# Narrow zero fills around the last pair's first decay, and expert 0's first product ahead of the branch

## The chip, the core and the metric

The kernel runs on one core of one Trainium2 chip. A core has five engines that work side by side and meet only through semaphores: PE (TensorE: matrix products and transposes), DVE (VectorE), ACT (ScalarE), POOL (GpSimd) and SP (SyncE, which here does nothing but issue DMAs). Each engine takes its instructions in the order of its own queue. The metric is the time of one execution on the device in microseconds (us), as the median of several runs.

## The reference

A gated linear recurrence is followed by a mixture of experts that keeps at most 80 tokens per expert:

```
a_t   = exp(8 * sigmoid(r_gate) * log(clip(sigmoid(a_param))))          # x, r_gate, i_gate: 4 x 5056 x 256
xg    = sqrt(max(1 - a_t * a_t, 1e-6)) * sigmoid(i_gate) * x
h     = a_t[:, t] * h + xg[:, t];  y[:, t] = h                            # for t in range(5056), float32

x = y.reshape(20224, 256);  logits = x @ w_gate                           # 8 experts
expert = argmax(logits);  gate = softmax(logits)[expert]
out = zeros(20224, 256)
for e in range(8):
    tok = the 80 tokens of expert e with the largest gate (all, if fewer)
    out[tok] = gate[tok] * (relu(x[tok] @ w1[e]) @ w2[e])                 # w1: 256 x 1024, w2: 1024 x 256
```

Nearly all of the 20.7 MB of `out` is zeros; only 640 rows of it are written by experts.

## The kernel before

**Tiles and units.** The 20224 tokens are cut into 20 pairs of 1024 tokens; pair 0 and the last pair, 19, are each worked in two units. The units of pair 19 are unit 20 (its tokens 0 to 511) and unit 21 (tokens 512 to 767); there are 22 units, 0 to 21. One big tile `Y` has 25 slots of 128 partitions x 2 x 1024 floats. A unit's three inputs are loaded into free slots, and its recurrence is computed in the slot of its own pair, `Y[:, p]`. The two index `h` of a slot is the half of the 256 channels.

**Order.** What every engine and SP do up to the routing is one list, `ORDER` (lines 31 to 51), written out by hand; each engine's queue has its own instructions in the order of that list. A letter is a step, followed by the unit and, after the point, the channel half: `r`, `i`, `x` issue the loads; `T` and `I` are the tanh of the gates on ACT (L117, L137); `A` transposes the r gate on PE into one PSUM buffer (L123); `E` is the decay, an exp on ACT from PSUM into the state `Y[:, p, h]` (L126); `Q` squares the decay on POOL (L129); `S` is the square root on ACT (L133), which needs another activation table than `E`; `U` multiplies gate and x on POOL (L140); `B` transposes that on PE (L147, L148); `N` scales it on DVE (L151); `Y` is the scan on DVE (L161), in place in the state; `l` computes the logits on PE (L241); `c` are the routing steps of a group of pairs (L245 to L271); `D` runs so many idle transposes on PE (L231); and `Z` issues a zero fill.

**Zero fills.** `zero_fill` (L203) writes the next rows of `out` with zeros from SBUF, by a DMA of SP's queue. Slot 19 is cleared once at the start. A wide fill (L209) writes 512 tokens, 512 KB, from all 1024 columns of `Y[:, 19, 0]`, 4 KB per partition. A narrow fill (L215) writes 256 tokens, 256 KB, from columns 768 to 1023 of the same row (`zero`), in pieces of 1 KB. No unit uses these columns, since the last pair has only 768 tokens. A wide fill reads where the decay `E20.0` will write. The flag `st['last']` is set when `E20.0` is put into the program; before it each `Z` is one wide fill, from then on two narrow ones. There are 28 wide and 23 narrow fills; the last narrow one is issued behind the first experts' weights.

**After the scans.** The routing picks each expert's best tokens: a chain of small DVE, POOL, ACT and PE steps up to `sel` (L449). Then `front` (L520) turns the choice into columns, keeps PE busy with 30 transposes (`keep_warm(WARM[3])`, L527, L352) and gathers the tokens of experts 0 and 1 into `XG`: `fetch` reads column numbers into registers (L505), and `copies` moves one token per instruction, 32 on ACT (L511), 24 on POOL and 24 on DVE (L512) for each expert. `rows_of_slots` (L513, five small DVE steps) follows. Ahead of `front` every engine reads a flag, and behind it there is a branch, `tc.If`: one side is a general way for many tokens in few rows, which is not taken here, the other is `experts` alone.

**Experts.** `experts` (L537) loops over `k`: `first(k)` is the product with `w1` into PSUM (L550, two halves), `relu(k, 0)` on ACT and `relu(k, 1)` on DVE write the hidden layer (L566, L565), `second(k)` is the product with `w2` (L560), `take` on ACT, `turn` on PE and `weigh` on DVE (L567, L571, L573) make rows, and `scatter` on POOL writes them (L576). In the same loop the tokens of expert `k + 2` are gathered and its weights loaded (L304, L307) into the buffers that expert `k` leaves.

Of the kernel before, what the change touches and what calls it, by code (L numbers as in the profile page):

```python
# [8 lines left out]
F32 = mybir.dt.float32  # L9
# [7 lines left out]
P = 128  # L17
# [26 lines left out]
A16.1 Z N15.0 D2 B15.1 E16.1 c2.1 c1.8 T17 Q16 l13 Y15.0 x17@23 Z I17 A17.0 N15.1 c2.2 B16.0 E17.0 r18@22 Y15.1 Z S16.1 A17.1 Z U17 c2.3 D4  # L44
B16.1 N16.0 l14 i18@24 E17.1 N16.1 x18@18 l15 T18 Y16.0 Q17 r19@20 c2.4 Y16.1 S17.1 D4 B17.0 c2.5 B17.1 N17.0 A18.0 i19@23 I18 c2.6 l16
N17.1 E18.0 U18 c2.7 c3.1 x19@21 c2.8 T19 A18.1 Z Y17.0 Z c3.2 Z E18.1 Z c3.3 I19 Q18 Y17.1 D14 B18.0 Z c3.4 Z c3.5 S18.1 B18.1 U19 c3.6
A19.0 i20@24 l17 N18.0 E19.0 N18.1 c3.7 Y18.0 D3 A19.1 r20@22 r21@22 E19.1 Z Z Z c3.8 Q19 D8 B19.0 I20 Z Y18.1 T20 T21 t D4 B19.1 S19.1 l18
x20@21 Z Z Z A20.0 Z Z E20.0 D9 A20.1 U20 i21@24 N19.0 E20.1 x21@21 N19.1 Z D5 A21.0 E21.0 Q20 Y19.0 Z S20.1 Z Y19.1 D23 B20.0 Z A21.1
E21.1 I21 N20.0 Z Q21 D5 B20.1 S21.1 c4.1 Y20.0 l19 U21 Z N20.1 c4.2 B21.0 Z Y20.1 c4.3 Z D5 B21.1 N21.0 l20 c4.4 N21.1 Y21.0 Z Y21.1 c4.5
D4 l21 Z c4.6 Z D2 c4.7 c5.1 c4.8 D2 c5.2 c5.3 c5.4 c5.5 c5.6 D25 c5.7 D7 c5.8  # L50
"""

def read_order():
# [11 lines left out]
def moe_kernel(ctx, tc, x, r_gate, i_gate, a_param, w_gate, w1, w2, out, capacity=80):  # L65
# [56 lines left out]
            at = 2 * g + (c0 - g) * D + h * P  # L122
            nc.tensor.transpose(pr[:, c0:min(n, g + 512):nb], rr[:, at:at + P], ident)  # L123
    def decay(u, h):
        if UNITS[u][0] == PAIRS - 1: st['last'] = True
        nc.scalar.activation(state(u, h), prs.pop((u, h))[:, :UNITS[u][2]], AF.Exp, scale=L[:, h:h + 1], bias=L[:, h:h + 1])  # L126
    def square(u):
        a = state(u)
# [74 lines left out]
    def zero_fill(k, wide=False):  # L203
        for _ in range(k):
            a = nz[0]
            if a >= N: return
            if wide and N - a >= 512 and not st.get('last'):
                nz[0] = a + 512
                nc.sync.dma_start(out[a:a + 512].rearrange("(p b) d -> p (b d)", p=P), Y[:, PAIRS - 1, 0])  # L209
                continue  # L210
            if wide:
                zero_fill(2)
                continue
            b = min(N, a + ZERO_TOKENS); nz[0] = b; m = (b - a) * D // P // ZC
            nc.sync.dma_start(out[a:b].rearrange("t d -> (t d)").rearrange("(p m c) -> p m c", m=m, c=ZC),  # L215
                              zero.unsqueeze(1).broadcast_to([P, m, ZC]))
# [65 lines left out]
    def gate_weights():  # L282
# [2 lines left out]
    tasks = {'r': lambda u: load('r', u, rf), 'i': lambda u: load('i', u, jf), 'x': lambda u: load('x', u, xf),  # L285
             'A': r_transposes, 'T': r_tanh, 'E': decay, 'Q': square, 'S': root, 'I': i_tanh, 'U': gated,
             'B': u_transposes, 'N': normed, 'Y': scan, 'c': lambda s, k: stages[k](s, width(s)), 't': early_top,
             'l': logits, 'D': idle, 'Z': lambda: zero_fill(1, True), 'w': gate_weights}
    with tc.manual_schedule(engines={E_.Activation, E_.PE, E_.DVE, E_.Pool, E_.SP}):
        for kind, nums in order: tasks[kind](*nums)  # L290
    mstack.close()
# [211 lines left out]
    def fetch(k, e):  # L503
        eng, et, a, b = SPAN[k]
        regs[k] = nc.values_load_multi_w_load_instructions(col[e:e + 1, a:b], engines=[et], min_val=0, max_val=PAIRS * 2 * C - C - 1,  # L505
                                                           skip_runtime_bounds_check_because="a token's column")[1]
    def copies(k, e, j0=0, j1=64):
        eng, et, a, b = SPAN[k]
        for j in range(a + j0, min(b, a + j1)):
            src = flat[:, bass.ds(regs[k][j - a], 2, step=C)]; dst = XG[:, e % 4, :, j]  # L510
            if k == 'A': eng.copy(dst, src)  # L511
            else: eng.tensor_copy(dst, src)  # L512
    def rows_of_slots():  # L513

        nc.vector.tensor_scalar(tk, AT[:, :E], -1.0, 0.0, op0=ALU.add, op1=ALU.max)
        nc.vector.tensor_scalar(un, tk, 11, 10, op0=ALU.logical_shift_right, op1=ALU.logical_shift_left)
        nc.vector.tensor_tensor(tk, tk, un, op=ALU.subtract)
        nc.vector.tensor_scalar(none, AT[:, :E], 0.0, 65536.0, op0=ALU.is_equal, op1=ALU.mult)
        nc.vector.tensor_tensor(sidx, tk, none, op=ALU.add)
    def front(ps):  # L520

        pc = ps.tile([E, CAP], F32, name="pv")
        nc.tensor.matmul(pc, comb[:3 * V, :E], chosen, start=True, stop=True)
        nc.vector.tensor_scalar(col, pc, -1.0, 0.0, op0=ALU.add, op1=ALU.max)
        pt = ps.tile([CAP, 2 * E], F32, name="sel")
        nc.tensor.matmul(pt, chosen, comb[:3 * V], start=True, stop=True)
        keep_warm(WARM[3], ps)  # L527
        for k in 'APV': fetch(k, 0)
        for k in 'APV': copies(k, 0)
        nc.vector.tensor_copy(AT, pt)  # L530
        for k in 'APV': fetch(k, 1); copies(k, 1)
        rows_of_slots()
    _, fv = nc.values_load_multi_w_load_instructions(flag, engines=[E_.PE, E_.DVE, E_.Activation, E_.Pool, E_.SP], min_val=0, max_val=P,
                                                     skip_runtime_bounds_check_because="a count of rows")
    with tc.manual_schedule(engines={E_.Activation, E_.PE, E_.DVE, E_.Pool, E_.SP}): front(ps_t)
    tstack.close()
    def experts(own):  # L537

# [4 lines left out]
        phs, pos, outs, sent = {}, {}, {}, []
        def hidden(e): return hbuf[e % 2].rearrange("p (c s) -> p c s", c=FC)
        def first(e, half):
            ph = phs[e, half] = ps_f.tile([P, FC // 2, CAP], F32, name="ph", bufs=3)
            for c in range(half * FC // 2, (half + 1) * FC // 2):
                for h in range(2):
                    for j in range(0, P, P // 2):
                        nc.tensor.matmul(ph[j:j + P // 2, c % (FC // 2)], w1v(e)[:, h, c * P + j:c * P + j + P // 2], XG[:, e % 4, h],  # L550
                                         start=(h == 0), stop=(h == 1), tile_position=(0, j))
            if half and e + 2 < E:
                for g in range(2): load_w1(e + 2, g)
# [9 lines left out]
        def relu(e, half):  # L563
            dst = hidden(e)[:, half * FC // 2:(half + 1) * FC // 2]
            if half: nc.vector.tensor_scalar_max(dst, phs.pop((e, half)), 0.0)  # L565
            else: nc.scalar.activation(dst, phs.pop((e, half)), AF.Relu)  # L566
        def take(e): nc.scalar.copy(turned[e % 2], pos.pop(e)[:, :, :CAP])  # L567
        def turn(e):

            outs[e] = ps_f.tile([CAP, 2 * P], F32, name="pd")  # L570
            for h in range(2): nc.tensor.transpose(outs[e][:, h * P:h * P + P], turned[e % 2][:, h], ident)  # L571
        def weigh(e):
            nc.vector.tensor_scalar_mul(res[e % 4][:CAP], outs.pop(e), AT[:, E + e:E + e + 1])  # L573
        def scatter(e):

            ins = nc.gpsimd.indirect_dma_start(out=out, out_offset=bass.IndirectOffsetOnAxis(ap=sidx[:, e:e + 1], axis=0),  # L576
                                               in_=res[e % 4][:CAP], in_offset=None, bounds_check=N - 1, oob_is_err=False)
            for other in sent: tc.declare_no_dep(ins.ins, other.ins, reason="rows of other tokens")
# [58 lines left out]
```

## Time and profile before

| what | value |
|---|---|
| median of 3 runs | 305.67 us (305.45 to 306.17) |
| the profiled execution: its time, its span | 306.08 us, 304.3 us |
| PE busy | 252.0 us (83% of the span) |
| ACT busy | 230.1 us (76%) |
| DVE busy | 210.5 us (69%) |
| POOL busy | 202.4 us (67%) |
| moved by DMA | 100.99 MB, mean 332 GB/s |

The times below are microseconds from the start of the span of the profiled execution. A row of the timeline gives start, duration, engine, line, operation, output and inputs, how many were merged, and in brackets the idle time of the engine before it and what ended that idle time. "SPq" is SP's queue: its rows are issues of DMAs, not the transfers. "issue" means that the profile shows nothing that the engine waited for. A row of the windows view gives, for one stretch, each engine's busy time, the clock granted to PE as a share of full speed, the busy share of the 16 DMA engines, and GB/s.

### The profile page before, as it was taken

The numbers are of one execution on the slowest core, as the hardware profiler recorded it, in microseconds if no ns is written. First come the engines' busy times: TensorE is split into PE (matmuls) and PEld (weight loads), VectorE is DVE, ScalarE is ACT, GpSimd is POOL, SyncE is SP. The second block draws the span as 40 slices with busy tenths as digits, with TensorE's granted clock in tenths as the row PEclk, the third lists the DMA queues.
The fourth block names the chain that finished last, engine by engine and source line by source line (L and its number), as shares of the span: only waits on it lengthen the run. The fifth ranks groups of instructions, "written<-read, shape, count | busy, mean of one in ns | idle before, by whom it ended". The sixth has DMA issues, their size and how long they took to land.

```text
span 304.3 us, 9900 instructions
## 1 busy us (share of the span) xinstructions
PE 252.0 (83%) x3748; PEld 228.0 (75%) x3748; DVE 210.5 (69%) x435; ACT 230.1 (76%) x443; POOL 202.4 (67%) x289
## 2 busy tenths in 40 slices
PE   4968899999899998999799798508979586996882
PEld 3767788898899897988788787407868486986871
DVE  2022069989999999999779889960779566566520
ACT  6999999999989999998998994607703366666510
POOL 2349999899999799899767488032305366777212
PEclk9999999999999999999999999955999787999997
DMA  6999999999999999889999999999997004999941
GB/s 235 407 412 408 409 411 407 408 408 408 407 416 412 365 364 323 325 313 381 409 357 401 310 369 416 408 363 329 308 346 259 1 4 167 300 382 384 360 150 32
DMA packets 38438, 100.99 MB, mean 332 GB/s; under 512 B 3056, under 2 KB 17264, under 8 KB 38384
## 3 DMA queue, kind: packets, MB, share of 16 engines
q1 hardware_dynamic: 38000, 99.63, 87.1%
q8 instruction: 31, 0.51, 0.7%
q0 software_dynamic: 384, 0.66, 0.7%
q14 instruction: 23, 0.19, 0.2%
HBM read 78.91 MB, written 21.36 MB: 330 GB/s over the span
## 4 chain that ended last, share of the span: by engine, by line
ACT 23%; DVE 18%; issue 14%; POOL 13%; DMA 12%; PE 11%; SPq 5%; POOLq 3%; DVEq 0%; ACTq 0%
DVE Y L161 8%; ACT Y L126 8%; POOL Y L512 6%; DVE pu L151 6%; ACT Y L117 5%; SPq L215 4%; ACT Y L133 4%; DMA out_dram<-Y 4%; DMA Y<-in_x_dram 4%; PE pr L123 3%; ACT Y L137 3%; POOLq L505 3%; DMA Y<-in_i_gate_dram 3%; POOL Y L129 2%; PE pu L147 2%
## 5 line engine op out<-in xcount | busy, mean ns | idle before, releaser
L140 POOL TENSOR_TENSOR Y<-Y 128x2048 f32<-128x2048 f32 (+2 forms) x22 | 90.9, 4142 | 20.7 <-DMA Y<-in_x_dram 14.4
L161 DVE TENSOR_TENSOR_SCAN Y<-Y,pu 128x1024 f32<-128x1024 f32 (+8 forms) x50 | 93.3, 1882 | 1.4 <-DMA out_dram<-Y 0.5
L129 POOL TENSOR_TENSOR Y<-Y 128x2048 f32<-128x2048 f32 (+2 forms) x22 | 71.6, 3260 | 28.7 <-ACT Y L126 18.7
L151 DVE SCALAR_TENSOR_TENSOR pu<-Y,pu 128x1024 f32<-128x1024 f32 (+2 forms) x44 | 48.6, 1111 | 52.8 <-PE pu L148 44.7
L148 PE MATMUL pu<-ident,Y 128*128 128x128 f32 x316 | 71.7, 274 | 3.4 <-POOL Y L140 3.4
L147 PE MATMUL pu<-ident,Y 128*128 128x128 f32 x316 | 72.6, 275 | 1.3 <-DVE Y L161 0.5
L123 PE MATMUL pr<-ident,Y 128*128 128x128 f32 x316 | 46.1, 289 | 24.3 <-ACT Y L126 20.0
L123 PEld LDWEIGHTS pr<-ident,Y 128*128 128x128 f32 x316 | 35.8, 146 | 32.6 <-ACT Y L126 27.7
L126 ACT ACTIVATE Y<-pr,tiny 128x1024 f32<-128x1024 f32 (+2 forms) x44 | 49.0, 1113 | 5.6 <-PE pr L123 5.3
L147 PEld LDWEIGHTS pu<-ident,Y 128*128 128x128 f32 x316 | 44.6, 141 | 4.8 <-issue 2.3
L148 PEld LDWEIGHTS pu<-ident,Y 128*128 128x128 f32 x316 | 44.6, 141 | 4.6 <-POOL Y L140 4.6
L231 PE MATMUL pl<-ident 128*128 128x128 f32 x287 | 42.6, 295 | 2.4 <-POOL ident masks.py:199 1.6
L137 ACT ACTIVATE Y<-Y 128x2048 f32<-128x2048 f32 (+2 forms) x22 | 38.2, 1736 | 4.7 <-DMA Y<-in_i_gate_dram 4.6
L511 ACT COPY Y<-Y 128x2 f32 x256 | 26.5, 191 | 18.5 <-issue 10.2
L117 ACT ACTIVATE Y<-Y 128x2048 f32<-128x2048 f32 (+2 forms) x22 | 38.1, 1736 | 2.7 <-DMA Y<-in_r_gate_dram 2.7
L241 PE MATMUL pl<-Y 128*32 128x64 f32 (+2 forms) x1344 | 39.0, 280 | 1.1 <-DVE lg L245 1.1
L231 PEld LDWEIGHTS pl<-ident 128*128 128x128 f32 x287 | 36.5, 154 | 3.2 <-POOL ident masks.py:199 1.6
L133 ACT ACTIVATE Y<-Y 128x2048 f32<-128x2048 f32 (+2 forms) x22 | 37.4, 1734 | 0.7 <-POOL Y L129 0.6
L241 PEld LDWEIGHTS pl<-Y 128*32 128x32 f32 x1344 | 33.9, 124 | 4.6 <-issue 3.2
L512 POOL COPY Y<-Y 128x2 f32 x192 | 24.4, 198 | 11.5 <-issue 6.9
L512 DVE COPY Y<-Y 128x2 f32 x192 | 22.6, 176 | 12.0 <-issue 12.0
L550 PE MATMUL ph<-Y 128*64 128x80 f32 x512 | 20.5, 233 | 4.9 <-issue 4.8
(126 smaller groups left out, 221.9 us busy)
## 6 DMA issues: line engine op xcount, KB each, us to landing
Y<-in_r_gate_dram SPq DMA_DIRECT2D x18, 1024.0 KB, 12.1
Y<-in_x_dram SPq DMA_DIRECT2D x18, 1024.0 KB, 9.3
Y<-in_i_gate_dram SPq DMA_DIRECT2D x18, 1024.0 KB, 9.7
Y<-in_moe_w_dram SPq DMA_DIRECT2D x32, 512.0 KB, 7.2
out_dram<-Y SPq DMA_DIRECT2D x28, 512.0 KB, 9.9
out_dram<-Y SPq DMA_DIRECT2D x23, 256.0 KB, 4.5
Y<-in_r_gate_dram SPq DMA_DIRECT2D x3, 512.0 KB
Y<-in_i_gate_dram SPq DMA_DIRECT2D x3, 512.0 KB
```

What stands on the lines that cost most here:

```text
L117: nc.scalar.activation(r, r, AF.Tanh, scale=0.5)
L123: nc.tensor.transpose(pr[:, c0:min(n, g + 512):nb], rr[:, at:at + P], ident)
L126: nc.scalar.activation(state(u, h), prs.pop((u, h))[:, :UNITS[u][2]], AF.Exp, scale=L[:, h:h + 1], bias=L[:, h:h + 1])
L129: nc.gpsimd.tensor_tensor(halves('r', u), a, a, op=ALU.mult)
L140: nc.gpsimd.tensor_tensor(i, i, flat('x', u), op=ALU.mult)
L147: nc.tensor.matmul(cols, xx[:, at:at + P], ident, start=True, stop=False, is_transpose=True)
L148: nc.tensor.matmul(cols, ii[:, at:at + P], ident, start=False, stop=True, is_transpose=True)
L151: nc.vector.scalar_tensor_tensor(pu, halves('r', u)[:, h], 0.5e-3, pu, op0=ALU.max, op1=ALU.mult)
L161: nc.vector.tensor_tensor_scan(y[:, s0:s1], y[:, s0:s1], q[:, s0:s1], init, op0=ALU.mult, op1=ALU.add)
L231: for _ in range(n): nc.tensor.transpose(spare, ident, ident)
L241: nc.tensor.matmul(pl[32 * j:32 * j + 32, s % 2, c0:c0 + n // NR], gates(h, b), Y[:, p, h, o + 4 * j + b:o + n:NR], start=(b == 0 and h == ...
L512: else: eng.tensor_copy(dst, src)
```

## The change

The nine `Z` that stand between the loads `r21` and the decay `E20.0` in the order, and all behind it, become `z`: two narrow fills each. The flag `st['last']` goes away; a `Z` is always a wide fill. So nine wide fills become eighteen narrow ones, and the fills behind `E20.0` are narrow as before.

In `front`, `rows_of_slots` moves ahead of the gather of expert 1, `first(0)` and `relu(0)` are computed there, between the gather of expert 0 and that of expert 1, and `keep_warm` runs 26 transposes in place of 30. The hidden layer of expert 0 goes to columns 1024 to 1663 of slot 24 (`scr`) in place of `rows`; its PSUM tile comes from the pool in front of the branch. The loop in `experts` skips `first` and `relu` for expert 0, and issues the loads of `w1` from the loop body.

```diff
-WARM = (4, 45, 6, 30)
+WARM = (4, 45, 6, 26)
...
-A19.0 i20@24 l17 N18.0 E19.0 N18.1 c3.7 Y18.0 D3 A19.1 r20@22 r21@22 E19.1 Z Z Z c3.8 Q19 D8 B19.0 I20 Z Y18.1 T20 T21 t D4 B19.1 S19.1 l18
-x20@21 Z Z Z A20.0 Z Z E20.0 D9 A20.1 U20 i21@24 N19.0 E20.1 x21@21 N19.1 Z D5 A21.0 E21.0 Q20 Y19.0 Z S20.1 Z Y19.1 D23 B20.0 Z A21.1
-E21.1 I21 N20.0 Z Q21 D5 B20.1 S21.1 c4.1 Y20.0 l19 U21 Z N20.1 c4.2 B21.0 Z Y20.1 c4.3 Z D5 B21.1 N21.0 l20 c4.4 N21.1 Y21.0 Z Y21.1 c4.5
+A19.0 i20@24 l17 N18.0 E19.0 N18.1 c3.7 Y18.0 D3 A19.1 r20@22 r21@22 E19.1 z z z c3.8 Q19 D8 B19.0 I20 z Y18.1 T20 T21 t D4 B19.1 S19.1 l18
+x20@21 z z z A20.0 z z E20.0 D9 A20.1 U20 i21@24 N19.0 E20.1 x21@21 N19.1 z D5 A21.0 E21.0 Q20 Y19.0 z S20.1 z Y19.1 D23 B20.0 z A21.1
+E21.1 I21 N20.0 z Q21 D5 B20.1 S21.1 c4.1 Y20.0 l19 U21 z N20.1 c4.2 B21.0 z Y20.1 c4.3 z D5 B21.1 N21.0 l20 c4.4 N21.1 Y21.0 z Y21.1 c4.5
...
-        if UNITS[u][0] == PAIRS - 1: st['last'] = True
...
-            if wide and N - a >= 512 and not st.get('last'):
+            if wide and N - a >= 512:
...
+             'l': logits, 'D': idle, 'Z': lambda: zero_fill(1, True), 'z': lambda: zero_fill(2), 'w': gate_weights}
...
+    hbuf = [rows[:, :FC * CAP], rows[:, FC * CAP:2 * FC * CAP], scr[:, 1024:1024 + FC * CAP]]
+    def hidden(e): return hbuf[e % 2 if e else 2].rearrange("p (c s) -> p c s", c=FC)
...
-        for k in 'APV': fetch(k, 1); copies(k, 1)
         rows_of_slots()
+        for half in range(2): first(0, half, ps, 2)
+        for k in 'APV': fetch(k, 1)
+        for half in range(2): relu(0, half)
+        for k in 'APV': copies(k, 1)
...
-            if k: take(k - 1)
-            if 0 < k < E - 1: copies('A', g - 1, 16, 24)
-            first(k, 0); relu(k, 0)
-            if 0 < k < E - 1: copies('A', g - 1, 24); copies('V', g - 1, 20)
-            first(k, 1); relu(k, 1)
-            if k: turn(k - 1); weigh(k - 1)
+            if k:
+                take(k - 1)
+                if k < E - 1: copies('A', g - 1, 16, 24)
+                first(k, 0, ps_f, 3); relu(k, 0)
+                if k < E - 1: copies('A', g - 1, 24); copies('V', g - 1, 20)
+                first(k, 1, ps_f, 3); relu(k, 1)
+                turn(k - 1); weigh(k - 1)
             if g < E:
+                for h in range(2): load_w1(g, h)
                 for q in 'APV': fetch(q, g)
                 copies('A', g, 0, 16); copies('V', g, 0, 20); copies('P', g)
```

`first` and `relu` keep their bodies; `first` gets the PSUM pool and its number of buffers as arguments.

## Rows read from the trace of the kernel before

**Rows 1.** The page: GB/s in 40 equal slices of the span.

```profile
GB/s 235 407 412 408 409 411 407 408 408 408 407 416 412 365 364 323 325 313 381 409 357 401 310 369 416 408 363 329 308 346 259 1 4 167 300 382 384 360 150 32
```

**Rows 2.** The timeline from 193 to 222 us, units 20 and 21.

```profile
197.94 2.34 POOL L140 TENSOR_TENSOR Y<-Y 128x1024 f32<-128x1024 f32 x1 [7.89 <-DMA Y<-in_x_dram]
...
204.75 1.28 ACT L126 ACT_TABLE_LOAD   x1 [9.06 <-DMA out_dram<-Y]
...
208.94 1.89 POOL L129 TENSOR_TENSOR Y<-Y 128x1024 f32<-128x1024 f32 x1 [8.66 <-issue]
...
211.47 1.06 ACT L133 ACTIVATE Y<-Y 128x1024 f32<-128x1024 f32 x1
...
213.32 0.27 PE L147 MATMUL pu<-ident,Y 128*128 128x128 f32 x1
...
214.46 0.69 DVE L151 SCALAR_TENSOR_TENSOR pu<-Y,pu 128x512 f32<-128x512 f32 x1 [11.89 <-PE pu L148]
214.62 0.56 ACT L126 ACTIVATE Y<-pr,tiny 128x256 f32<-128x256 f32 x1 [0.79 <-PE pr L123]
...
215.08 0.62 ACT L137 ACTIVATE Y<-Y 128x512 f32<-128x512 f32 x1
...
216.62 1.30 POOL L140 TENSOR_TENSOR Y<-Y 128x512 f32<-128x512 f32 x1
217.01 0.63 ACT L133 ACTIVATE Y<-Y 128x512 f32<-128x512 f32 x1
...
219.25 0.30 PE L147 MATMUL pu<-ident,Y 128*128 128x128 f32 x1
```

**Rows 3.** The timeline of SP's queue from 184 to 226 us.

```profile
184.46 2.98 SPq L209 DMA_DIRECT2D out_dram<-Y  x4
189.78 0.34 SPq L109 DMA_DIRECT2D Y<-in_x_dram  x1
190.17 4.61 SPq L209 DMA_DIRECT2D out_dram<-Y  x5
195.25 0.53 SPq L113 DMA_DIRECT2D Y<-in_i_gate_dram  x1
196.53 0.39 SPq L113 DMA_DIRECT2D Y<-in_x_dram  x1
197.74 21.71 SPq L215 DMA_DIRECT2D out_dram<-Y  x22
219.55 1.05 SPq L304 DMA_DIRECT2D Y<-in_moe_w_dram  x2
```

**Rows 4.** Tile Y, loads of unit 21 (195 to 197 us): from issue to landing.

```profile
DMA to landing us min/median/max: 9.5/9.8/10.1
```

**Rows 5.** Line L215, fills from 199 and from 207.8 us: ns of an issue, landing.

```profile
L215 SPq DMA_DIRECT2D out_dram<-Y x5: 933/1318/1543, 199.0 to 204.8; - x5
...
L215 SPq DMA_DIRECT2D out_dram<-Y x12: 680/716/737, 207.8 to 216.1; - x12
...
DMA to landing us min/median/max: 3.8/3.9/4.4
```

**Rows 6.** Windows: engines busy, PE clock, DMA share, GB/s.

```profile
184.40:197.00 12.60, 9.42 (x128) 8.34 (x126) 12.19 (x16) 7.04 (x6) 4.92 (x3) 1.00 1.02 411
207.00:219.00 12.00, 12.00 (x131) 11.32 (x131) 4.03 (x5) 9.29 (x11) 4.34 (x4) 0.78 0.99 330
```

**Rows 7.** The timeline from 247 to 262 us, experts 0 and 1.

```profile
247.94 2.43 PE L550 MATMUL ph<-Y 128*64 128x80 f32 x64 [0.19 <-issue]
...
249.57 3.33 ACT L511 COPY Y<-Y 128x2 f32 x32 [1.83 <-PE ph L550]
...
253.19 0.44 ACT L566 ACTIVATE rows<-ph 128x320 f32<-128x320 f32 x1 [0.29 <-issue]
...
253.68 3.88 PE L560 MATMUL po<-rows,Y 128*64 128x80 f32 x64 [3.31 <-ACT rows L566]
...
257.61 0.29 ACT L567 COPY Y<-po 128x160 f32<-128x160 f32 x1 [0.61 <-PE po L560]
```

More of the change, by code (lines that the diff above doesn't have):

```diff
@@ L46 @@
 N17.1 E18.0 U18 c2.7 c3.1 x19@21 c2.8 T19 A18.1 Z Y17.0 Z c3.2 Z E18.1 Z c3.3 I19 Q18 Y17.1 D14 B18.0 Z c3.4 Z c3.5 S18.1 B18.1 U19 c3.6
-A19.0 i20@24 l17 N18.0 E19.0 N18.1 c3.7 Y18.0 D3 A19.1 r20@22 r21@22 E19.1 Z Z Z c3.8 Q19 D8 B19.0 I20 Z Y18.1 T20 T21 t D4 B19.1 S19.1 l18
-x20@21 Z Z Z A20.0 Z Z E20.0 D9 A20.1 U20 i21@24 N19.0 E20.1 x21@21 N19.1 Z D5 A21.0 E21.0 Q20 Y19.0 Z S20.1 Z Y19.1 D23 B20.0 Z A21.1
-E21.1 I21 N20.0 Z Q21 D5 B20.1 S21.1 c4.1 Y20.0 l19 U21 Z N20.1 c4.2 B21.0 Z Y20.1 c4.3 Z D5 B21.1 N21.0 l20 c4.4 N21.1 Y21.0 Z Y21.1 c4.5
-D4 l21 Z c4.6 Z D2 c4.7 c5.1 c4.8 D2 c5.2 c5.3 c5.4 c5.5 c5.6 D25 c5.7 D7 c5.8
+A19.0 i20@24 l17 N18.0 E19.0 N18.1 c3.7 Y18.0 D3 A19.1 r20@22 r21@22 E19.1 z z z c3.8 Q19 D8 B19.0 I20 z Y18.1 T20 T21 t D4 B19.1 S19.1 l18
+x20@21 z z z A20.0 z z E20.0 D9 A20.1 U20 i21@24 N19.0 E20.1 x21@21 N19.1 z D5 A21.0 E21.0 Q20 Y19.0 z S20.1 z Y19.1 D23 B20.0 z A21.1
+E21.1 I21 N20.0 z Q21 D5 B20.1 S21.1 c4.1 Y20.0 l19 U21 z N20.1 c4.2 B21.0 z Y20.1 c4.3 z D5 B21.1 N21.0 l20 c4.4 N21.1 Y21.0 z Y21.1 c4.5
+D4 l21 z c4.6 z D2 c4.7 c5.1 c4.8 D2 c5.2 c5.3 c5.4 c5.5 c5.6 D25 c5.7 D7 c5.8
 """
@@ L287, in moe_kernel @@
              'B': u_transposes, 'N': normed, 'Y': scan, 'c': lambda s, k: stages[k](s, width(s)), 't': early_top,
-             'l': logits, 'D': idle, 'Z': lambda: zero_fill(1, True), 'w': gate_weights}
+             'l': logits, 'D': idle, 'Z': lambda: zero_fill(1, True), 'z': lambda: zero_fill(2), 'w': gate_weights}
     with tc.manual_schedule(engines={E_.Activation, E_.PE, E_.DVE, E_.Pool, E_.SP}):
@@ L519, in rows_of_slots, with first, relu @@
         nc.vector.tensor_tensor(sidx, tk, none, op=ALU.add)
+    hbuf = [rows[:, :FC * CAP], rows[:, FC * CAP:2 * FC * CAP], scr[:, 1024:1024 + FC * CAP]]
+    phs = {}
+    def hidden(e): return hbuf[e % 2 if e else 2].rearrange("p (c s) -> p c s", c=FC)
+    def first(e, half, ps, bufs):
+        ph = phs[e, half] = ps.tile([P, FC // 2, CAP], F32, name="ph", bufs=bufs)
+        for c in range(half * FC // 2, (half + 1) * FC // 2):
+            for h in range(2):
+                for j in range(0, P, P // 2):
+                    nc.tensor.matmul(ph[j:j + P // 2, c % (FC // 2)], w1v(e)[:, h, c * P + j:c * P + j + P // 2], XG[:, e % 4, h],
+                                     start=(h == 0), stop=(h == 1), tile_position=(0, j))
+    def relu(e, half):
+        dst = hidden(e)[:, half * FC // 2:(half + 1) * FC // 2]
+        if half: nc.vector.tensor_scalar_max(dst, phs.pop((e, half)), 0.0)
+        else: nc.scalar.activation(dst, phs.pop((e, half)), AF.Relu)
     def front(ps):
@@ L539, in experts @@
         ps_f = own.enter_context(tc.tile_pool(name="ps_f", bufs=1, space=bass.MemoryType.PSUM))
-        hbuf = [rows[:, :FC * CAP], rows[:, FC * CAP:2 * FC * CAP]]
         turned = [scr[:, (8 + 2 * k) * CAP:(10 + 2 * k) * CAP].rearrange("p (h s) -> p h s", h=2) for k in range(2)]
         res = [scr[:, 1024:1280], scr[:, 1280:1536], scr[:, 1536:1792], scr[:, 1792:2048]]
[L543 to L553, printed above, removed]
+        pos, outs, sent = {}, {}, []
         def second(e, half):
@@ L562, in second @@
             if e + 2 < E: load_w2(e + 2, half)
[L563 to L566, printed above, removed]
         def take(e): nc.scalar.copy(turned[e % 2], pos.pop(e)[:, :, :CAP])
```

## The prediction

> **What bounds the kernel now.** I read the page's GB/s line first [rows 1]. Up to about 190 us every slice but the first stands between 310 and 416 GB/s; the transfers set the pace there, and the change leaves that stretch alone. From 236 to 251 us the line shows 1 and 4 GB/s: the transfers have run dry, and the kernel is a chain of small computing steps that nothing but their own start can shorten. So the question is what decides when that chain starts. It starts with the last scans, those of units 20 and 21, so the next view is the timeline from 193 to 222 us [rows 2].
>
> There ACT is idle for 9.06 us, to 204.75, and what ends it is a transfer to `out`. The table load behind the wait is that of the decay `E20.0`, which writes the part of slot 19 that the wide fills read. ACT had been free since 195.69 (204.75 - 9.06). Behind it everything of unit 20 is late: POOL idles 8.66 us before `Q20` at 208.94, DVE 11.89 us before `N20.0` at 214.46. SP's queue [rows 3] shows the nine wide fills, four issued from 184.46 and five from 190.17, around the load `x20`, then `i21` and `x21`, then 22 narrow ones one after another to 219.45.
>
> The last view is the timeline around the branch [rows 7]. PE ends `first(0)` at 250.37 (247.94 + 2.43) and begins `second(0)` at 253.68, 3.31 us later, released by `relu(0, 0)`. That stands behind the 32 copies of expert 1 on ACT's queue, which began at 249.57.
>
> **The change part by part.**
>
> *The wait of the decay.* With the fills from the columns 768 to 1023, no transfer behind the r loads reads what `E20.0` writes. The wide fills that remain ahead of it are issued before `r21`, and so ahead of the 184.46 of [rows 3]; with 10.1 us to landing, the longest of [rows 4], they are in by 194.6. `E20.0`'s table load can begin when ACT is free, at 195.69: a gain of 9.06 us at this step. From there to `B20.0` (213.32) the path is decay, transposes, idle transposes on ACT and PE, and moves as a block: `B20.0` at 204.26, and `N20.0`, whose transposes end just ahead of it, at 205.40.
>
> *What is late next.* Two things could hold up this block. The first is `x20`, which POOL waits for at 197.94 before `U20` (2.34 us), with `Q20` behind it in the queue. Four wide fills ahead of it become eight narrow ones. A pair of narrow fills moves the same 0.524 MB as a wide one. At 411 GB/s, the rate of the stretch with wide fills, that is 1.28 us; at 330 GB/s, the stretch of narrow ones [rows 6], it is 1.59. Four times the difference of 0.31 is 1.25 us. `x20` lands at 199.2, `U20` ends at 201.5, `Q20` (1.89) at 203.4, the root `S20` (1.06 [rows 2]) at 204.5. `N20.0` needs it at 205.40: 0.9 us to spare, so this costs nothing.
>
> The second is `i21` and `x21`. They land 10.1 and 9.5 us after their issue [rows 4], at 205.35 and 206.03, behind all nine. At 0.31 each they come 2.8 us later, at 208.15 and 208.8. ACT is ready for `I21` at 206.4 (`E21.1` before: 214.62 + 0.56 [rows 2]; less 9.06 it would end at 206.1; behind the root at 204.5 and a table load of 1.28 it ends at about 206.4), so now `I21` waits for its load: it ends at 208.8 in place of 215.70. `U21` then begins at 208.9 (before: 216.62), the root `S21` about 210.1 (217.01). The last transposes `B21.1` stood 2.63 us behind the start of `U21`, at 219.25, released by the scan of unit 20; that scan now ends 9.06 earlier, so `U21` decides: 208.9 + 1.30 for itself and about 1.1 for eight transposes of its first half and the idle ones gives 211.3, a gain of 8.0. That is the lower end. The upper comes from the issue of narrow fills in a full stream, 716 ns each [rows 5]: two are 1.43 us, nine pairs cost 9 x 0.15 = 1.4 us, `x21` lands at 207.4, and the gain is all of 9.06. The row of 330 GB/s holds thin moments that the second one has not; I take the middle, **8.5 us**.
>
> On rate the Trainium skill (DMA: Bandwidth & Descriptors, Specifications) gives 512 B as the smallest transfer for line rate, and pieces of 1 KB are above that. By that rule the fills would cost nothing, and this step would give 9.06. The trace says otherwise: 330 against 411 GB/s [rows 6].
>
> *What the narrow fills push back.* The first weights were issued at 219.55 [rows 3], behind all fills, and come 1.4 to 2.8 us later. `first(0)` used them at 247.94, now at about 239.4; landing within 10.1 us of the issue, the longest of [rows 4], they would be there by 232.5. The dry stretch from 236 [rows 1] covers that. Without this cover every microsecond would be paid.
>
> *From the scans to the gather* no instruction is changed, and the chain moves as it is.
>
> *The product and relu ahead of the branch.* `first(0)` still waits for the last copy of expert 0 on ACT, which ended at 247.74 (249.57 - 1.83 [rows 7]); PE began at 247.94. Four idle transposes fewer therefore give nothing, and cost nothing as long as PE's clock stays up. The two relus come ahead of the copies of expert 1. ACT reaches its own after `fetch`, at 249.57, with the first half of the product (half of 2.43) done at 249.2; DVE's follows the second half at 250.4 and takes about 0.5, so `second(0)` may begin at about 250.9: 2.7 us earlier. But ACT's queue holds the same work as before, with relu (0.44) and copies (3.33) exchanged. `take(0)` stands behind `fetch` and copies for expert 2, and only its own wait for PE, 0.61 us at 257.61, goes away. `relu(1, 0)` is behind it, and with that `second(1)`. So of 2.7 us PE keeps 0.6. DVE's copies of expert 1 come later by five small steps and a relu, some 2 us; the product that needs them comes behind `second(0)`, which took 3.88, so from 254.8. They meet it closely; the loss, if any, is that 0.6 and some tenths. Bounds: 0 and 2.7; I take **0.6**, the row of ACT's wait.
>
> *At nothing:* `load_w1` keeps its place in SP's queue, and for expert 2 it still waits for `first(0)`. The new place of the hidden layer overlaps the buffers that `weigh(0)` writes, but that comes behind `second(0)` in any case.
>
> The sum against the profiled execution: 306.08 - 8.5 - 0.6 = 297.0. That execution was 0.41 us above the median of the runs, 305.67; against the median it is **296.6 us**.
>
> **The rivals.**
>
> *The fills eat most of it.* The rate of narrow fills is not all: five of the issues took a median of 1.32 us and up to 1.54 [rows 5], while wide ones and loads were still ahead of them. The 22 of [rows 3] took 0.99 each. Eighteen at that are 17.8 us against 7.6 for the nine wide, 10.2 later. But the loads then stand in a shorter queue and land in 4.4 us rather than 10.1 [rows 4, 5], so `i21` is 4.5 later, at 209.9, and `x21` near 210.5. `U21` starts at 210.6, the gain falls to 6.2, and the time is 298.9 with the second edit's 0.6, 299.5 without. It decides when `x21` lands later than 208.8. At 1.54 for every one of the eighteen (27.7 us, 20.1 later) `x21` would land near 221, 4.4 after `U21`'s start before, and the time would be 309.5: one of the rivals on the slow side.
>
> On many small transfers the Trainium skill (DMA: Bandwidth & Descriptors, Anatomy of one DMA, told there for the path of GpSimd) counts some 2 us fixed for each. Paid in a row by nine more fills that is an estimate of 18 us, close to the 20.1 of this slow end. The rows show issues 0.72 us apart that land after 3.9 [rows 5]: they overlap, and the cost is not paid one by one.
>
> *PE keeps the lead.* If ACT is not what holds `second(1)`, all of 2.7 us stays: 305.67 - 8.5 - 2.7 = 294.5. Against it stands the 0.61 us of [rows 7]: ACT had hardly any waiting to lose.
>
> *The second edit loses its gain*, since the copies of expert 1 come late: 0 in place of 0.6, up to 1 lost; 297.2 to 298.2.
>
> *Slower: the wait stays and grows.* The narrow fills read the same row `Y[:, 19, 0]` as the wide ones, at other columns. If the waits are set for the row and not for the columns, `E20.0` waits for the eighteenth narrow fill, which lands 1.4 to 2.8 us later than the ninth wide one did, near 207.5 in place of 204.75. With 0.6 from the second edit that gives 307.9. Below 0.6 us of delay it would be no change. The rows don't decide between the two readings: whatever writes this row behind the 22 narrow fills of [rows 3] comes late enough for those ahead of it to have landed. The program names columns that don't overlap, and I hold it unlikely.
>
> **How the numbers follow.** What this measurement can tell from no change is about 0.2%, 0.6 us. The forecast, 296.0 (9.06) to 297.1 (8.0) and 0.6 to either side, so 295.4 to 297.7, has a chance of 0.55. The fills eating most of it has 0.18 (298 to 301), their slow end 0.02, PE keeping the lead 0.1 (294 to 295.4), the second edit losing its gain 0.08 (297.2 to 298.6), the wait that stays 0.05, and 0.02 is left for no change. The prediction is that of the forecast, 296.6. To leave out no more than 2 in 10 the range runs from 294.4 to 300.0. Faster by more than 0.2% is 0.91 (0.55, 0.18, 0.1 and 0.08), within it 0.02, slower 0.07.
>
> **What would show it right or wrong.** In the profile after, ACT's idle time before the table load of `E20.0` should be nearly gone, with `E20.0` at about 197. `I21` should be released by its load, at about 207 to 208.2, and `N20.0` begin near 205.4. The last `B21.1` should be near 210.3 to 211.3. `second(0)` should begin within 0.7 us of the end of `first(0)`, and `second(1)` be released by ACT. The forecast is wrong if `E20.0` is still released by a transfer to `out`, if `x20` lands after 200.1 (the spare 0.9 us gone), if `first(0)` waits for weights, or if the gaps of PE in the later experts grow.

## The result, and the profile after

| what | before | changed |
|---|---|---|
| median of 4 runs | 305.92 us (305.45 to 307.17) | 294.47 us (291.80 to 295.59) |
| ratio, 95% interval | | 0.961 (0.954 to 0.968) |
| the profiled execution: time, span | 306.08, 304.3 us | 295.59, 293.8 us |

The change gains about 11.5 us by the medians, where 9.1 were forecast. The two profiled executions differ by 10.49 us. The means, standard errors and ratios below leave out runs more than 1.5% above the fastest of the same kernel in their group, the medians do not; with those runs in, no mean of the last table moves by more than 0.3 us. The timeline of the changed kernel over units 20 and 21 answers to [rows 2]:

```profile
195.72 1.28 ACT L125 ACT_TABLE_LOAD   x1
197.01 0.78 ACT L125 ACTIVATE Y<-pr,tiny 128x512 f32<-128x512 f32 x1
198.38 2.35 POOL L139 TENSOR_TENSOR Y<-Y 128x1024 f32<-128x1024 f32 x1 [8.63 <-DMA Y<-in_x_dram]
...
200.31 2.92 PE L230 MATMUL pl<-ident 128*128 128x128 f32 x23
...
202.61 1.06 ACT L132 ACTIVATE Y<-Y 128x1024 f32<-128x1024 f32 x1 [0.19 <-POOL Y L128]
...
204.20 0.70 DVE L150 SCALAR_TENSOR_TENSOR pu<-Y,pu 128x512 f32<-128x512 f32 x1 [1.62 <-PE pu L147]
...
205.88 0.63 ACT L136 ACTIVATE Y<-Y 128x512 f32<-128x512 f32 x1 [0.34 <-DMA Y<-in_i_gate_dram]
...
206.71 1.29 POOL L139 TENSOR_TENSOR Y<-Y 128x512 f32<-128x512 f32 x1
...
208.98 0.27 PE L146 MATMUL pu<-ident,Y 128*128 128x128 f32 x1
```

The table load of `E20.0` has no idle time before it any more; it begins at 195.72, which is 9.03 us earlier than in [rows 2]. `N20.0` begins at 204.20 (10.26 earlier), `I21` at 205.88, released by its load after 0.34 us. The last `B21.1` begins at 208.98 (10.27 earlier). The timeline of SP's queue, which answers to [rows 3]:

```profile
184.09 8.15 SPq L214 DMA_DIRECT2D out_dram<-Y  x8
192.35 0.99 SPq L109 DMA_DIRECT2D Y<-in_x_dram  x1
193.39 8.04 SPq L214 DMA_DIRECT2D out_dram<-Y  x10
201.47 0.70 SPq L113 DMA_DIRECT2D Y<-in_i_gate_dram  x1
202.26 0.63 SPq L113 DMA_DIRECT2D Y<-in_x_dram  x1
202.94 17.29 SPq L214 DMA_DIRECT2D out_dram<-Y  x22
220.32 1.38 SPq L303 DMA_DIRECT2D Y<-in_moe_w_dram  x2
```

`i21` is issued 6.2 us later than before and lands only some 0.5 later. Line L113's loads from 201 to 203 us:

```profile
DMA to landing us min/median/max: 4.3/4.4/4.4
```

Issue to landing is 4.4 us, against 9.5 to 10.1 in [rows 4]. The later issue and the shorter way to landing nearly cancel. PE's timeline around the branch answers to [rows 7]:

```profile
238.10 2.43 PE L527 MATMUL ph<-Y 128*64 128x80 f32 x64 [1.49 <-DVE lg L517]
240.62 2.44 PE L565 MATMUL po<-Y 128*64 128x80 f32 x64
243.75 2.43 PE L527 MATMUL ph<-Y 128*64 128x80 f32 x64 [0.69 <-DVE Y L511]
247.51 0.42 PE L572 MATMUL pd<-ident,Y 128*80 128x128 f32 x2 [1.33 <-ACT Y L568]
248.60 4.05 PE L565 MATMUL po<-rows,Y 128*64 128x80 f32 x64 [0.67 <-ACT rows L532]
252.48 2.38 PE L527 MATMUL ph<-Y 128*64 128x80 f32 x64
```

`second(0)` stands directly behind `first(0)` and takes 2.44 us; in [rows 7] it took 3.88 after a gap of 3.31. But in this execution `second(1)`, with the same 64 matmuls, takes 4.05. The windows view, columns as in [rows 6], shows why: first the stretch of `second(1)`, then `first(0)` to `first(2)`, and last the same stretch of the kernel before.

```profile
248.60:252.48 3.88, 3.88 (x64) 3.88 (x66) 2.58 (x19) 2.30 (x24) 2.67 (x21) 0.56 0.66 207
...
238.10:252.48 14.38, 11.60 (x258) 10.92 (x260) 8.65 (x69) 8.68 (x83) 9.19 (x72) 0.88 0.69 225
247.94:262.31 14.37, 11.06 (x259) 10.62 (x260) 8.05 (x60) 8.24 (x75) 9.15 (x72) 0.88 0.51 163
```

The granted clock is 0.56 in the first row: most of this product ran at the lower level (1.2 GHz). So the execution profiled here shows the first edit's gain and hardly any of the second's: from `first(0)` to `first(2)` it took 14.38 us, and the kernel before 14.37 (247.94 to 262.31). The difference between the kernels' medians is larger than that of these two executions, and the experiments had to show from where.

### The profile page after: what moved, and what is told of

The parts are those of the page before. It is cut to its first block, busy times and chain, and to the rows that moved or that the text cites. A ratio compares the mean times of both kernels' runs of the same rounds, so it can differ in the third digit from the quotient of the medians.

```text
span 293.8 us, 9900 instructions
## 1 busy us (share of the span) xinstructions
PE 250.0 (85%) x3744; PEld 227.2 (77%) x3744; DVE 210.2 (72%) x435; ACT 229.5 (78%) x443; POOL 202.2 (69%) x289
## 4 chain that ended last, share of the span: by engine, by line
ACT 28%; PE 17%; issue 14%; DVE 12%; POOL 12%; DMA 11%; POOLq 3%; ACTq 1%; SPq 1%; DVEq 0%
ACT Y L125 8%; ACT Y L132 6%; DVE Y L160 5%; POOL Y L511 5%; ACT Y L117 5%; PE pr L123 4%; DMA Y<-in_r_gate_dram 4%; DVE pu L150 4%; DMA Y<-in_x_dram 4%; DMA Y<-in_i_gate_dram 3%; PE pu L146 3%; PE pu L147 3%; ACT Y L136 3%; ACT L125 3%; PE pl L240 3%
```

## The experiments

The kernel before ran beside each group of experiments. Over all groups, the runs of the first table with them, its mean is 305.33 us (standard error 0.19), that of the changed kernel 293.81 (0.29). Both vary by some microseconds from run to run, so single microseconds below come from such means.

**Each edit alone, and the price of narrow fills.** `fills_only` is the kernel before with the fills' edit; `product_only` is the changed kernel with the old order and flag; `after_again` is the changed kernel unaltered, on the same chip; `all_narrow` makes every wide fill of the order narrow, 19 more.

```diff
 # fills_only, on the kernel before                       # in ORDER from r21@22 on: Z -> z
-        if UNITS[u][0] == PAIRS - 1: st['last'] = True
-            if wide and N - a >= 512 and not st.get('last'):
+            if wide and N - a >= 512:
 # all_narrow, on the changed kernel                      # in all of ORDER: Z -> z
-... i11@13 D7 B7.0 Y6.1 I9 A9.1 Z
+... i11@13 D7 B7.0 Y6.1 I9 A9.1 z
```

> The fills alone; expert 0's product stays behind the branch and 30 idle transposes are kept. Theory A (the forecast's first term was too small: the narrow fills hold the loads back by half a microsecond and not by 1.4 to 2.8, and the rest of the gain is PE's clock in this stretch): 9.8 us less than before, which is where first(0) stood in the profile after, so about 296.1. Theory B (the first term was right at 8.5, the second edit gives the rest): about 297.4.

> The product and relu ahead of the branch alone, the fills wide as before. Theory A (ACT's queue gives the lead back within two experts): 0.6 us less than before, 305.3. Theory B (PE keeps the lead of about 3 us that second(0) has): near 302.8.

> The changed kernel unchanged, for a closer interval on the same chip as the two halves. If the halves add up, its gain over before is the sum of theirs, 10.4 by theory A of both; if it is near 12, something is gained only by both together.

> The changed kernel with the 19 wide fills that remain made narrow as well, 38 of them in the stretch where transfers set the pace. Theory A (a pair of narrow fills costs 1.36 us where a wide one costs 1.25, as the landings in the profile after show): 19 x 0.11 = 2.1 us more than the changed kernel. Theory B (the 330 GB/s of the forecast): 19 x 0.31 = 5.9 us more.

| kernel | median us | ratio to before, 95% |
|---|---|---|
| fills_only | 296.20 | 0.969 (0.964 to 0.973) |
| product_only | 303.09 | 0.988 (0.982 to 0.994) |
| after_again | 292.88 | 0.959 (0.954 to 0.963) |
| all_narrow | 294.22 | 0.963 (0.958 to 0.969) |

Both edits gain alone, and the two gains add up: 9.4 (305.56 - 296.20) and 2.5 us make 11.9, and together they give 12.7. The second edit is worth several times the 0.6 us forecast. Nineteen more fills in two pieces cost 1.3 us by these medians, some 0.07 each, and 0.6 ± 0.6 by the means over all runs (294.44 less 293.81); the forecast had 0.15 to 0.31 for one.

The windows view from `first(0)` to `first(2)`, first `fills_only`, then `after_again`:

```profile
238.27:253.88 15.61, 12.29 (x259) 11.85 (x261) 8.05 (x60) 8.24 (x75) 9.63 (x73) 0.78 0.50 157
```

```profile
235.64:248.39 12.75, 9.98 (x258) 9.29 (x260) 7.32 (x58) 7.20 (x69) 8.61 (x69) 1.00 0.73 247
```

The same work, in another order, takes 15.61 us with a granted clock of 0.78 and 12.75 with 1.00. That brought up the next question: is the gain of the second edit its order, as I had forecast, or that it closes the gap behind `first(0)`, after which PE's clock is down?

**PE kept busy without the new order.** `fills_warm` is `fills_only` with 28 idle transposes in the gap behind `first(0)`, `before_warm` is the kernel before with the same; the transposes compute nothing that is used. `after_warm` puts 12 into the changed kernel, behind `first(1)`. `relu_late` moves the relus of expert 0 behind the copies of expert 1, so that the gap before `second(0)` is there again. `fills_late` takes out the nine `z` between `r21` and `E20.0`; the last fill, behind the weights of the first experts, then writes those rows too.

```diff
 # fills_warm, before_warm (28, for k == 0, behind first and relu) and after_warm (12, for k == 1, ahead of turn)
+        def busy(n):
+            pw = ps_f.tile([P, 2 * P], F32, name="pd")
+            for _ in range(n): nc.tensor.transpose(pw[:, :P], ident, ident)
+            if k == 0: busy(28)
 # relu_late, on the changed kernel
-        for half in range(2): relu(0, half)
         for k in 'APV': copies(k, 1)
+        for half in range(2): relu(0, half)
 # fills_late, on the changed kernel: the nine z go
-... r20@22 r21@22 E19.1 z z z c3.8 Q19 D8 B19.0 I20 z Y18.1 ... x20@21 z z z A20.0 z z E20.0
+... r20@22 r21@22 E19.1 c3.8 Q19 D8 B19.0 I20 Y18.1 ... x20@21 A20.0 E20.0
```

> The changed kernel with relu(0) behind the copies of expert 1 again; the product stays ahead of the branch. Theory A (the second edit's gain comes from letting second(0) begin before those copies): second(0) goes back to about 15.9 us behind the start of the gather, as before (253.68 - 237.7), and the time to that of the fills alone, near 296. Theory B (it comes from the product's place ahead of the branch): within 1 us of the changed kernel, near 293.

> The fills alone, with 28 idle transposes on PE between first(0) and second(0), which keep PE busy over the 3.3 us in which it waits for the relu; they compute nothing that is used. Theory A (of the 3.3 us by which the second edit made the kernel faster, most is that PE does not fall to half clock in this gap, so second(0) takes 2.43 and not 3.9 to 4.5): 1.5 to 2 us less than the fills alone, near 294.5. Theory B (it is the earlier start of second(0) itself): no change from the fills alone, near 296.

> The changed kernel with 12 idle transposes on PE between first(1) and turn(0), where PE waited 1.3 us for ACT; they compute nothing that is used. Theory A (runs of this kernel differ by where PE's half clock falls, and this gap is one such place): the slowest of the runs comes down and the median falls by 0.3 to 0.8. Theory B (the runs differ for another reason): no change.

> The changed kernel without the nine pairs of narrow fills ahead of the decay; the same zeros are written by narrow fills behind the first weights. Theory A (the narrow fills hold back the loads of units 20 and 21 by some 0.5 us against wide ones): x20, i21 and x21 land about 12 us earlier, but ACT and PE already set the pace, so Q20 begins 0.9 earlier at most and the time falls by 0.3 to 0.6. Theory B (the loads' lateness is what is left of the wait): 2 us or more less. If the fills behind the weights are in the way of the later loads, it is slower.

> The kernel before with nothing changed but 28 idle transposes on PE between first(0) and second(0); they compute nothing that is used. Theory A (what the second edit brings is mostly PE's clock in the experts): 1.5 to 2.5 us less than before, without any earlier start of second(0), and 12.8 to 12.9 us from the start of first(0) to that of first(2) in place of 14.4. Theory B (it is the earlier start): no change.

| kernel | median us | ratio to before, 95% |
|---|---|---|
| relu_late | 294.55 | 0.969 (0.963 to 0.975) |
| fills_warm | 295.01 | 0.968 (0.961 to 0.975) |
| after_warm | 293.27 | 0.965 (0.958 to 0.971) |
| fills_late | 296.00 | 0.972 (0.965 to 0.978) |
| before_warm | 303.68 | 0.994 (0.990 to 0.997) |

Without any change of the order, 28 transposes gain 1.6 us on the kernel before (305.29 there). PE's timeline, `fills_only` first and then `before_warm`:

```profile
244.02 4.54 PE L559 MATMUL po<-rows,Y 128*64 128x80 f32 x64 [3.32 <-ACT rows L565]
```

```profile
249.87 3.27 PE L570 MATMUL pd<-ident 128*128 128x128 f32 x28
...
253.25 2.44 PE L560 MATMUL po<-rows,Y 128*64 128x80 f32 x64
```

The windows view of `before_warm` over `first(0)` to `first(2)`:

```profile
247.50:260.44 12.94, 12.83 (x287) 12.22 (x288) 8.05 (x60) 7.71 (x72) 8.91 (x70) 1.00 0.59 192
```

`second(0)` begins no earlier behind `first(0)`, and yet takes 2.44 us in place of 4.54. With the transposes, `first(0)` to `first(2)` is 12.94 us in `before_warm` and 12.91 in `fills_warm`, at a granted clock of 1.00; the changed kernel and its variants at full clock take 12.75 to 12.78. There the new order is therefore worth 0.15 us in this stretch.

`relu_late` shows the other side. PE's timeline:

```profile
236.14 2.44 PE L527 MATMUL ph<-Y 128*64 128x80 f32 x64 [1.67 <-DVE lg L517]
241.64 2.44 PE L565 MATMUL po<-Y 128*64 128x80 f32 x64 [3.07 <-ACT Y L532]
```

The gap is back, 3.07 us, but here the clock stayed up, and `first(0)` to `first(2)` took 12.78. So the place of the relu costs nothing up to there as long as the clock holds (the mean of its runs, 294.62 ± 0.51, is not clearly above the changed kernel's); and a gap of 3 us is not always followed by the lower level.

`fills_late` was to be faster if the eighteen fills ahead of unit 21's loads still cost much. Its last scan does come earlier, ending 13.87 us behind the start of `E20.0`, against 14.33 to 15.45 in the four profiled executions of the changed kernel. But it is slower than the changed kernel. SP's queue, then ACT's timeline at the gather:

```profile
217.03 19.24 SPq L214 DMA_DIRECT2D out_dram<-Y  x19
```

```profile
238.01 3.13 ACT L510 COPY Y<-Y 128x2 f32 x32 [9.81 <-POOL Y L511]
```

The routing's choice is ready at 230.61, and the gather starts on POOL only at 236.64, 0.37 us behind the end of the last issue of a fill (217.03 + 19.24). In the changed kernel it starts on ACT at 234.87 and on POOL at 234.55, for a choice at 231.26. I take it that SP, which must come to the flag ahead of `front` as the other engines do, is still in its fills; this was not tried by itself.

**What the clock costs elsewhere.** `after_cold` leaves 2 idle transposes ahead of `first(0)` in place of 26. `after_busy` puts 28 more between `A20.0` and `A20.1`, where PE waits in the first edit's stretch. `after_third` is the changed kernel again.

```diff
-WARM = (4, 45, 6, 26)                  # after_cold
+WARM = (4, 45, 6, 2)
-x20@21 z z z A20.0 z z E20.0 D9 A20.1  # after_busy
+x20@21 z z z A20.0 z z E20.0 D37 A20.1
```

> The changed kernel with 2 idle transposes ahead of first(0) in place of 26, so that PE idles for some 5 us before it. Theory A (the clock): first(0) and second(0) run at half clock, and the time is 1.5 to 2.5 us above the changed kernel. Theory B (the order): first(0) still begins with the last copy of expert 0, and the time stays within 0.5 us.

> The changed kernel as it is, beside the others on this chip: 293.3, the mean of its ten runs so far, within 1 us.

> The changed kernel with 37 idle transposes in place of 9 on PE between A20.0 and A20.1, where PE waits for the decay for 4 us; they compute nothing that is used. Theory A (the stretch from E20.0 to the last scan became 1 us shorter than before because PE's half clock ends earlier in it, and some 0.5 us of half clock is left): from E20.0's start to the end of the last scan 13.9 us in place of 14.3 to 14.7, and up to 0.5 us off the time. Theory B (that stretch is bound by loads and POOL): no change.

| kernel | median us | ratio to before, 95% |
|---|---|---|
| after_cold | 293.71 | 0.964 (0.959 to 0.969) |
| after_third | 294.04 | 0.967 (0.962 to 0.972) |
| after_busy | 295.68 | 0.968 (0.963 to 0.973) |

For both new kernels theory A, the clock, missed, and B came nearer. `after_cold` shows no loss (mean 293.79 ± 0.56, `after_third` beside it 294.36 ± 0.59), though its `first(0)` takes 4.53 us and its `second(0)` 3.23: its `second(1)` then runs at full clock, and from `first(0)` to `first(2)` it takes 14.01 us, inside the 12.75 to 14.38 of the changed kernel's own executions. `after_busy` shows no gain (295.07 ± 0.51). In its timeline `N20.0` is released by the square root on ACT and no longer by PE:

```profile
205.16 0.70 DVE L150 SCALAR_TENSOR_TENSOR pu<-Y,pu 128x512 f32<-128x512 f32 x1 [0.53 <-ACT Y L132]
```

The 23 idle transposes run in 2.67 us there, but the chain of `x20` is now last, 8.58 us behind the table load (205.16 - 196.58). The changed kernel has 8.48 in the profile above. In this execution nothing is left for PE to give in that stretch; in other executions of the changed kernel there is, as shown further below.

**Both edits crossed.** The last four ran together on one chip: fills alone or the whole change, each without and with the idle transposes (28 and 12 as above).

> One of four on one chip, two orders by two clocks: the fills alone, PE idle between first(0) and second(0). By the earlier runs 296.3. If the second edit's 3.0 us is 1.7 of clock and 1.3 of order, the four stand at 296.3 (this), 294.7 (with idle transposes), 293.6 (the changed kernel), and 293.3 to 293.6 (the changed kernel with idle transposes).

> The fills alone with 28 idle transposes between first(0) and second(0). If clock and order share as above 294.7; if it is all clock 293.5, if all order 296.3.

> The changed kernel as it is: 293.7, the mean of its sixteen runs so far, whichever theory holds.

> The changed kernel with 12 idle transposes between first(1) and turn(0): 293.3 to 293.6. Its difference to the fills with idle transposes is what the order gives when the clock is kept up in both; the forecast said 0.6.

| kernel | median us | ratio to before, 95% |
|---|---|---|
| grid_fills | 295.52 | 0.966 (0.960 to 0.972) |
| grid_fills_warm | 293.47 | 0.962 (0.958 to 0.966) |
| grid_after | 293.65 | 0.963 (0.959 to 0.969) |
| grid_after_warm | 293.30 | 0.960 (0.956 to 0.964) |

The table of means over the runs of the same kernel, from all groups, has the smaller errors, but it mixes chips, and the transposes of its rows differ in number and place:

| | idle | with idle transposes | difference |
|---|---|---|---|
| before | 305.33 ± 0.19 | 303.31 ± 0.38 | 2.02 ± 0.42 |
| fills only | 295.68 ± 0.44 | 294.26 ± 0.34 | 1.42 ± 0.56 |
| the whole change | 293.81 ± 0.29 | 293.38 ± 0.17 | 0.43 ± 0.34 |
| fills only, less the whole | 1.87 ± 0.53 | 0.88 ± 0.38 | |

(± is the standard error.) The second edit is worth 1.9 us where nothing else keeps PE's clock up, and 0.9 where the transposes do. The difference of the two, 1.0 ± 0.7, is not clear of noise, and by the last four runs alone they are 0.9 ± 0.9 and 0.4 ± 0.3. In the windows view over `first(0)` to `first(2)`, `grid_after` and then `grid_after_warm`:

```profile
237.06:251.20 14.14, 11.37 (x258) 10.68 (x260) 8.42 (x68) 8.59 (x83) 9.21 (x72) 0.90 0.69 230
```

```profile
237.33:250.11 12.78, 11.41 (x270) 10.59 (x272) 7.33 (x59) 7.20 (x69) 8.69 (x69) 1.00 0.71 246
```

Of the four profiled executions of the changed kernel two have this stretch at a full clock (12.75, 12.76) and two not (14.14, 14.38); all five executions with transposes in the loop have it at full clock. Their times also scatter less: the whole change with 12 transposes has standard deviations of 0.4 and 0.7 us in its two groups of runs, without them 0.9 to 1.6. It is not faster than the changed kernel beyond doubt, and no version that ran is.

## Why the prediction was right or wrong

**The wait of the decay: right.** `E20.0`'s table load stands directly behind the root of unit 19, as worked out: 195.69 forecast, 195.72 in the profile, 9.03 us gained. The rival in which the wait stays is out.

**What is late next: the transfers, right in kind, too large at the landings.** `I21` is released by its load, as said, but at 205.88 and not at 207 to 208.2. The step that failed leads from the price of a pair of narrow fills to the landing of the loads behind it. Nine pairs at 0.15 to 0.31 us each were to put `i21` back by 1.4 to 2.8 us. It landed 0.53 later (205.88, before 205.35 as worked out in the prediction), which is 0.06 for each pair. `x20` was there at 198.38 at the latest, 0.44 later than before; from then to `i21` ten narrow fills and the load went by in 7.50 us, where five wide ones and the same load had taken 7.41.

The price itself was not refuted. The windows view from the first of these fills to the landing of `i21`, before and after:

```profile
184.46:205.35 20.89, 9.36 (x128) 8.28 (x125) 17.70 (x18) 7.64 (x7) 7.20 (x4) 0.84 1.00 395
184.09:205.88 21.79, 17.46 (x193) 16.02 (x195) 19.42 (x21) 14.62 (x14) 9.85 (x7) 0.92 1.02 361
```

With the DMA engines fully busy in both, the stretch with narrow fills moved 361 GB/s and the one with wide fills 395. The page's row of the queue that carries nearly all transfers gives its packets, MB and busy share of the 16 engines, before and after:

```profile
q1 hardware_dynamic: 38000, 99.63, 87.1%
q1 hardware_dynamic: 41600, 99.63, 91.3%
```

As time that is 265.0 us of the span of 304.3, and 268.2 of 293.8. In the three profiles of kernels with nine wide fills here it is 265.0 to 265.3, in the fourteen with nine pairs in their place 266.5 to 268.6. So nine pairs kept the DMA engines busy some 2.6 us longer, 0.3 each, as the forecast's dear end had it; but the loads landed only 0.53 later. Why they bore so little of it was not tried. By the rule of the Trainium skill (DMA: Bandwidth & Descriptors, Specifications) pieces of 512 B already reach line rate. The trace does not bear that out for the rate of these 1 KB pieces (361 against 395 GB/s), though the landings came nearer to it than to the forecast.

**The block that "moves as a block": 1.2 us shorter in this execution, by luck.** From the table load to `N20.0` it was 9.71 us in [rows 2] and is 8.48. All of it is in the 23 idle transposes ahead of `B20.0`. PE's timeline before:

```profile
209.34 4.14 PE L231 MATMUL pl<-ident 128*128 128x128 f32 x23
```

They took 4.14 us there and 2.92 after. The windows view shows the clock granted over them, before and after:

```profile
205.00:213.32 8.32, 6.44 (x34) 6.25 (x35) 0.00 (x0) 6.27 (x7) 1.89 (x1) 0.56 0.94 319
201.00:204.20 3.20, 3.20 (x32) 3.20 (x31) 1.58 (x2) 2.97 (x4) 1.58 (x1) 1.00 1.06 338
```

So in these two profiles 9.03 + 1.22 and nothing for the fills makes the gain at the last `B21.1`, 10.27, where 8.5 were forecast. But the 1.22 belongs to the executions and not to the edit. The same 23 transposes took 2.92, 3.90, 4.31 and 2.97 us in the four profiles of the changed kernel, and 4.14, 3.79 and 3.27 in the three of kernels with wide fills. From `after_again`:

```profile
197.56 3.90 PE L230 MATMUL pl<-ident 128*128 128x128 f32 x23
```

The whole block took 8.48 to 9.87 us in the former and 8.82 to 9.71 in the latter. To the end, `fills_only` measured 9.6 ± 0.5 us (305.33 - 295.68): the 9.06 of the wait, and little or nothing taken off it by the fills.

**The second edit: right in what it moves, wrong in size and reason.** `second(0)` begins directly behind `first(0)`, and `second(1)` is released by ACT's relu, as forecast. The step that failed is that of the product and relu: there ACT's queue fixes `second(1)`, and PE's 3.88 us for `second(0)` and the cost-free idle transposes "as long as PE's clock stays up" stood as given. 3.88 was itself a duration mostly at the lower clock. The windows view before shows it over `second(0)`:

```profile
253.68:257.39 3.71, 3.71 (x65) 3.71 (x66) 2.43 (x22) 1.61 (x16) 2.99 (x24) 0.59 0.20 68
```

At full clock the product takes 2.44 us, and it does so behind `first(0)` in the changed kernel, where the gap of 3.31 us is closed. Measured, the edit is worth 1.9 ± 0.5 us (3.0 ± 0.8 alone, 305.33 less the 302.33 of `product_only`). With PE kept busy by other means 0.9 ± 0.4 remains, within its error of the 0.6 forecast for the order, of which the stretch up to `first(2)` shows 0.15. The rest, 1.0 ± 0.7, is put down to the clock. That filling the gap without any change of order gains 1.4 to 2.0 us is shown twice, by `fills_warm` and `before_warm`. The Trainium skill (TensorE: Matmul & The Clock Gate, The HAM clock gate) says that the array's clock is held down by default and released by activity; the granted clock of 0.78 in `fills_only` and 1.00 in `fills_warm`, which differ only by the transposes, agrees. The rival "PE keeps the lead" gave the measured time, 294.5, by luck: ACT did hold `second(1)`, and its two terms, 8.5 and 2.7, were measured as 9.6 and 1.9.

**The sum.** The forecast time was 2.1 us too long (296.6 against 294.47): by the means some 1.1 in the first term (8.5 forecast, 9.6 measured) and 1.3 in the second (0.6 forecast, 1.9 measured).

**What was at nothing.** `first(0)` waited for no weights (it is released by DVE in the profile after). The later start of the first weights cost nothing that shows, though their cover is nearly gone. The page after, which answers to [rows 1]:

```profile
GB/s 231 411 408 409 409 411 408 409 408 407 409 412 406 388 339 377 353 289 292 414 403 346 414 302 384 402 334 349 343 337 317 368 41 366 210 328 393 379 110 33
```

The dry stretch was two slices, 1 and 4 GB/s; now it is one, at 41. A further delay of the weights would have little cover.

The loads of the later experts' weights were at nothing too (`load_w1`) or left out (`load_w2`). From 20 to 40 us behind the start of `first(0)` the DMA engines are fully busy in all eighteen profiles (share 1.01 to 1.06, 369 to 385 GB/s). The windows view of that stretch, before and after:

```profile
267.94:287.94 20.00, 16.09 (x404) 14.46 (x400) 12.17 (x89) 12.44 (x116) 12.43 (x76) 1.00 1.05 382
258.10:278.10 20.00, 16.76 (x431) 15.43 (x428) 12.85 (x94) 12.91 (x116) 12.06 (x76) 1.00 1.01 369
```

So the later experts can hardly be faster than these loads, and a gain ahead of them counts as far as it starts them earlier. The new order does that: SP issues the second weights of expert 2 at 241.98, 3.88 us behind the start of `first(0)`, where it was 8.18 before (256.12 - 247.94). In the executions with a full clock up to `first(2)`, the rest from there to the end took 40.2 to 41.7 us in four of the whole change and 41.1 to 42.5 in three with the old order. That may be what is left of the 0.9 us; earlier loads by themselves were not tried. The gaps of PE in these experts did not grow: it was busy 16.09 of 20 us before and 16.76 after.

**Open.** Why the loads bore so little of the price of the narrow fills; why a gap of 3 us is followed by the lower clock in most executions and not in `relu_late`'s; and how much of the 0.9 us is order beyond the 0.15 seen up to `first(2)`.

## What to carry to other kernels

A duration of PE read behind a gap is a duration at the clock of that gap: before it enters a sum, look at the granted clock of its stretch, and price the removal of the gap at the full clock. A lower rate of transfers is not yet a later load: take the delay from the landings of the loads that something waits for. What differs between two profiled executions need not come from the edit: look at the same row in further executions of the same kernel. And a later issue need not be a later landing: here 6.2 us of the one were 0.5 of the other.

## What the runs showed that was not expected

- A product of 64 matmuls that takes 2.44 us at full clock took 3.88 to 4.54 behind a gap of some 3 us in three profiles (`before`, `fills_only`, `grid_fills`), and 2.44 in a fourth (`relu_late`). Idle transposes that take 3.27 us in that gap delay nothing and give the difference back.
- Where the low clock falls differs from execution to execution of the same kernel (14.38 against 12.75 us in the same stretch). The spread of some 2 to 4 us between runs of a group was smaller with 12 transposes in the loop, but much of it lies elsewhere: in the four profiled executions of the changed kernel the table load of `E20.0`, which now waits for nothing but the work ahead of it, began between 193.43 and 196.20, and `first(0)` between 235.64 and 238.77.
- With nineteen fills on SP's queue behind the weights (`fills_late`) the gather began 6.0 us after the choice on POOL and 7.4 on ACT, against 3.3 and 3.6 in the changed kernel, though no engine needs a fill's data there. The cause was not tried.
